# A linear-attention kernel with a rational activation on one core: all steps in a new order, and about twenty steps on other engines

## The chip, the core and the metric

The kernel runs on one core of one Trainium2 chip. Times are device microseconds of one execution. The kernel before took 216.31, 215.97 and 213.47 us in the three runs shown, a median of 215.97 us. The profile is of one further execution.

The engines are named as the profile names them: PE multiplies matrices (PEld is its loading of weights), DVE is VectorE, ACT is ScalarE, POOL is GpSimd, SP only issues transfers. "L500" is line 500 of the kernel's file.

## The reference

For each of 4 batches and 8 heads, a state of 48 x 48 is carried over 768 time steps:

```python
f = 1.0 / (1.0 + np.exp(-f_logit))
for t in range(S):
    state = f[:, :, t, :, None] * state + np.einsum('bhd,bhe->bhde', k[:, :, t], v[:, :, t])
    y[:, :, t] = np.einsum('bhd,bhde->bhe', q[:, :, t], state)
```

The result, as 3072 tokens of 384 numbers (8 heads x 48), goes through two dense layers (384 to 2048 and back) with a rational activation between them:

```python
h = x @ w_in
P = a[0] + a[1] * h + a[2] * h**2 + a[3] * h**3
Q = 1.0 + abs(b[0]) * abs(h) + abs(b[1]) * h**2
out = (P / (Q + 1e-6)) @ w_out
```

## The kernel before

**Units.** The work is cut into 12 units, numbered 0 to 11. Unit n holds 256 time steps (n // 4 says which of three stretches) of batch n % 4, all eight heads. Units of one batch depend on each other through a state in SBUF; the four batches alternate, so there are three other units between a state's update and its next use. Within a unit the 256 steps are two chunks (j = 0, 1) and the heads are four pairs.

**Steps of a unit, attention.** `ld` loads f, k, q (issued by SP) and v (by POOL). `ef` and `ls` (ACT) make the logarithm of the gate; `cs` (PE) sums it over time; `A` (ACT) makes its exponentials; `xa` (DVE) multiplies q (x = 0) and k (x = 1) with them, or `xg` does it on POOL for half of k's heads. `T` (PE) transposes the products and `Te` (ACT, or DVE) copies the transposes to SBUF. `sc` (PE) makes the scores, `mk` (DVE) masks them, `yb` and `yi` (PE) make the attention output y from scores and from the old state, `kv` and `si` (PE) the new state, which `st` (DVE) scales. `vm` (POOL) packs a part of v for `yb`. `ye` copies y from PSUM to the tile xT (ACT with argument s, DVE with v).

**Steps of a unit, dense layers.** `h` (PE) multiplies with w_in, four blocks of 128 columns at a time, so four times a unit; `hy` copies each such group from PSUM to SBUF (ACT, or DVE with v). On the 16 blocks of a unit, DVE then squares (`sq`, L500), takes the absolute value (`ab`, L508), makes two affine forms (`p1`, L542, and `p2`, L547) and the product of one with the square (`pm`, L556). Two sums are left: the denominator's z + h2 and the numerator's g + hy. Each is made in halves of eight blocks (128 partitions x 2048 numbers), and each half in one of three ways: on DVE (`zv` L526, `tv` L564), by a DMA that accumulates in SBUF, issued by POOL (`zd` L530, `ta` L560), or, for some groups of the denominator, by PE (`u` L516). ACT takes the logarithm of the denominator (`ln` from PSUM, `lz` L534 from SBUF) and the exponential of its negative (`ex` L538), which gives 1/Q; DVE multiplies it in (`gm`, L568). `o` (PE, L578) multiplies with w_out, eight groups of four matmuls a unit, `oe` copies the result from PSUM, `so` stores it.

**What sets the order.** Nothing is scheduled. The text ORDER lists every step of all units in one order, and each engine works its own instructions in exactly that order, waiting on semaphores for what they need. `@2` gives the PSUM slot (of four). `>mk.2.0` after a load or an `xg` makes it wait for that other step. `dz` are matmuls without a use, in the first microseconds and at the end. POOL and SP are queues of the same kind: a transfer that waits for its buffer holds up whatever stands behind it. The tiles of q, k, f and v come from pools of three buffers each; a load waits until the last reader of the buffer's former contents is done.

The functions `load` (L184), `xa` (L305), `ye` (L433), `hy` (L493), `zv`, `zd`, `ta`, `tv` (L524 to L564) and `oe` (L581) are those that the steps named in the prediction run through.

Of the kernel before, what the change touches and what calls it, by code (L numbers as in the profile page):

```python
# [19 lines left out]
ld 0 f 2 4; cu 1; cz 0; ab_ b a; ld 0 f 0 2; cz 2; ld 0 k 0 2; cu 0; ld 0 k 2 4; ld 0 q 2 4; ci; cm; dz 9 @0  # L20
ld 0 q 0 2; ld 1 f; ld 0 v; ab_ a s; ld 1 k; fa; ld 1 q; ef 0 2 4; ef 0 0 2; cz 3; ls 0 0 2; ls 0 2 4; cz 1
cs 0 2 4 @2; cs 0 0 2 @3; A 0 0 2 4; dz 4 @0; A 0 1 2 4; xa 0 0 2 4; A 0 1 0 2; xa 0 1 2 4; A 0 0 0 2
xa 0 1 0 2; T 0 2 4 @0; vm 0 1; Te 0 2 4; dz 2 @2; sc 0 1 @0; kv 0 @3; xa 0 0 0 2; mk 0 1; T 0 0 2 @1; fr; ef 1
Te 0 0 2; dz 4 @2; ae 0; ls 1; wi 8 12; si 0 0; sc 0 0 @0; wi 12 16 >ls.1; ld 2 f >mk.0.1; vm 0 0; cs 1 @1
ld 1 v; yb 0 2 4 @2; mk 0 0; wi 4 8; st 0 0; A 1 1; wi 0 4; yb 0 0 2; xa 1 1; yi 0 1; si 0 1; dz 3 @0; A 1 0
xa 1 0; dz 3; st 0 1; ye 0 0 1 v; ye 0 1 3 s; T 1 @1; Te 1 s; vm 1 1; fb; vm 1 0; ld 2 v; h 0 8 12 @2
hy 0 8 12 v; vm 2 1; sc 1 0 @0; ef 2; sc 1 1 @3; vm 2 0; mk 1 1; ha 0 12 16 @1; hb 0 12 16; ld 3 f >ye.0.0.1
ls 2; kv 1 @2; si 1 0; dz 1 @3; cs 2 @3; hy 0 12 16; ae 1; mk 1 0; ld 2 k; yb 1 2 4 @0; ab 0 8 12; ld 3 v
yb 1 0 2; st 1 0; A 2 1; yi 1 1; si 1 1; ld 4 v; sq 0 8 12; A 2 0; h 0 4 8 @1; ye 1 s; ef 3; h 1 12 16 @3
# [12 lines left out]
sq 2 0 16; u 1 0 4 @3; gm 0 0 8; A 5 0; A 5 1; h 3 0 4 @2; wo 4 8; xg 5 1 0 2 >gm.0.0.8; hy 3 8 12; sc 4 1 @1
ln 1 0 4; kv 4 @3; h 3 12 16 @0; hy 3 0 4; ae 4; ex 1 8 16; ld 6 v; mk 4 1; ld 7 f; ld 9 f; ld 5 v; hy 3 12 16
xa 5 0; ef 6; ex 1 0 8; ld 6 k; si 4 0; o 0 0 0 4 @2; sc 4 0 @1; o 0 0 8 12; pm 2 0 16; h 3 4 8 @0; ls 6
xg 5 1 2 4 >pm.2.0.16; hy 3 4 8; mk 4 0; o 0 1 12 16; o 0 1 0 4; st 4 0; yb 4 2 4 @1; ef 7; zv 2 8 16; yi 4 1
yi 4 0; p2 2 0 16; lz 2 8 16; si 4 1; sq 3 0 16; o 0 0 12 16; yb 4 0 2; o 0 1 8 12; st 4 1; cs 6 @0; o 0 1 4 8
ab 3 0 16; o 0 0 4 8; ta 2 0 8; p1 3 0 16; ye 4 s; A 6 1; oe 0 0 2 s; A 6 0; h 4 4 8 @1; tv 1 8 16; T 5 @2
u 2 0 4 @3; hy 4 4 8; vm 6 0; ld 8 f; ef 9; ld 7 k; ld 8 v; h 4 12 16 @0; Te 5 s; ln 2 0 4; h 4 0 4 @1
hy 4 12 16; sc 5 0 @3; hy 4 0 4; h 4 8 12 @2; u 2 4 8 @1; ef 8; kv 5 @0; hy 4 8 12; ln 2 4 8; vm 5 1; pm 3 0 16
sc 5 1 @2; zd 3 0 8; vm 5 0; vm 6 1; si 5 0; so 0 0 2 s; gm 1 0 8; gm 1 8 16; o 1 1 4 8 @1  # L50
xg 6 1 0 2 >gm.1.8.16; mk 5 0; o 1 1 8 12; ae 5; xg 6 1 2 4 >mk.5.0; mk 5 1; ls 7; st 5 0; yi 5 0 @3; p2 3 0 16
ex 2 8 16; cs 7 @2; A 7 1; ld 6 q; ld 7 q; si 5 1; xa 6 0; yb 5 2 4; yb 5 0 2; yi 5 1; o 1 0 12 16; o 1 1 12 16
A 7 0; zv 3 8 16; ab 4 0 16; ex 2 0 8; T 6 @2; o 1 1 0 4; o 1 0 4 8; Te 6 s; ta 3 0 8; o 1 0 0 4; st 5 1
# [54 lines left out]
def kernel(  # L108
# [161 lines left out]
    def ef(n, a0=0, a1=HP):  # L270
        f = unit(n)["f"][:, 2 * a0:2 * a1].rearrange("p h i d -> p (h i d)")
        nc.scalar.activation(f, f, AF.Exp, scale=-1.0)  # L272
# [364 lines left out]
```

## Time and profile before

| | |
|---|---|
| runs shown | 216.31, 215.97, 213.47 us |
| span of the profiled execution (first to last instruction) | 212.2 us |
| the profiled execution's own time beside it | not given; the runs lie 1.3 to 4.1 us above the span |
| busy: PE, DVE, ACT, POOL | 202.0, 200.3, 193.2, 86.5 us |
| mean granted PE clock | 1.000 |
| moved by DMA | 41.10 MB |

A busy time counts from an instruction's start to its end. Neighbours on an engine overlap by a few hundredths of a microsecond, so what one instruction costs an engine without gaps is the distance from its start to the next one's. The ends of matmuls are modelled: one of 128x384 takes 326 ns by its row, but twelve in a row advance PE by 1.95 us. The DMA share of a stretch adds up the queues and can lie above 1.

### The profile page before, as it was taken

How to read it: one execution, taken by the hardware profiler on the slowest of the kernel's cores; microseconds unless marked ns; L12 is line 12 of the kernel's file. 1: busy time of each engine (PE TensorE's matmuls, PEld its weight loads, DVE VectorE, ACT ScalarE, POOL GpSimd, SP SyncE). 2: the span in 40 equal slices, each digit the busy share in tenths (PEclk: the TensorE clock that was granted, in tenths of full speed). 3: DMA queues.
4: the chain of work that ended last, by engine and by line, in shares of the span. 5: the costliest groups of instructions: out<-in, count | busy, mean ns of one | idle time of the engine just before them, and what ended most of it. 6: DMA issues, size and time to landing. Idle time of an engine off the chain costs nothing.

```text
span 212.2 us, 7141 instructions
## 1 busy us (share of the span) xinstructions
PE 202.0 (95%) x3167; PEld 140.4 (66%) x3167; DVE 200.3 (94%) x210; ACT 193.2 (91%) x195; POOL 86.5 (41%) x106
## 2 busy tenths in 40 slices
PE   4999999989999999999999999999999989999993
PEld 1466677557776675677686686686686667676551
DVE  4786989999999999999999999999999999999991
ACT  3565699999999999899999999999999999999990
POOL 6151222661324793633136447397356143133100
PEclk9999999999999999999999999999999999999999
DMA  5999999999899999999299999599997996949924
GB/s 138 244 200 215 233 241 223 255 235 214 152 187 74 237 207 240 259 197 213 73 237 238 238 235 182 97 191 244 201 189 150 186 173 117 198 89 274 204 116 153
DMA packets 60623, 41.10 MB, mean 194 GB/s; under 512 B 51120, under 2 KB 54960, under 8 KB 60592
## 3 DMA queue, kind: packets, MB, share of 16 engines
q0 software_dynamic: 20944, 21.76, 63.5%
q1 hardware_dynamic: 39360, 18.68, 34.1%
q8 instruction: 25, 0.41, 0.8%
q10 hardware_dynamic: 288, 0.20, 0.3%
q14 instruction: 6, 0.05, 0.1%
HBM read 25.17 MB, written 4.72 MB: 141 GB/s over the span
## 4 chain that ended last, share of the span: by engine, by line
PE 18%; ACT 16%; DVE 14%; issue 5%; DMA 4%; ACTq 0%; POOLq 0%
PE op L578 12%; PE hp L460 5%; ACT hy L495 4%; ACT qi L538 4%; DMA z<-h 4%; ACT lq L534 3%; DVE h L500 3%; DVE scm L359 2%; DVE gall L568 2%; ACT qkT L336 1%; DVE gall L542 1%; ACT A L303 1%; DVE z L508 1%; DVE gall L556 1%; DVE gall L564 1%
## 5 line engine op out<-in xcount | busy, mean ns | idle before, releaser
L578 PE MATMUL op<-w_out_sb,gall 128*128 128x384 bf16 x384 | 69.0, 326 | 0.0
L460 PE MATMUL hp<-xT,w_in_sb 128*128 128x256 bf16 x564 | 67.6, 273 | 1.4 <-ACT xT L442 0.7
L460 PEld LDWEIGHTS <-w_in_sb 128*128 128x128 bf16 x564 | 54.3, 98 | 11.2 <-issue 1.5
L578 PEld LDWEIGHTS <-gall 128*128 128x128 bf16 x384 | 36.2, 98 | 22.7 <-DVE gall L568 0.5
L495 ACT CAST hy<-hp 128x1024 bf16<-128x1024 f32 x47 | 49.3, 1090 | 1.1 <-PE hp L489 1.0
L538 ACT ACTIVATE qi<-lq 128x4096 bf16<-128x4096 f32 (+2 forms) x18 | 45.6, 2539 | 0.0
L534 ACT ACTIVATE lq<-z 128x2048 f32<-128x2048 bf16 (+1 forms) x20 | 36.8, 1878 | 0.3 <-DMA z<-h 0.3
L560 POOL DMA_DIRECT2D gall<-hy x18 | 19.3, 1124 | 28.4 <-DVE gall L556 10.8
L359 DVE TENSOR_TENSOR scm<-sc,mask 128x1024 bf16<-128x1024 f32 x24 | 28.8, 1217 | 0.6 <-PE sc L351 0.6
L314 POOL TENSOR_TENSOR qkp<-kn,A 128x384 bf16<-128x384 f32 x17 | 17.0, 1002 | 29.8 <-ACT alast L447 7.4
L500 DVE TENSOR_TENSOR h<-hy 128x4096 bf16<-128x4096 bf16 (+2 forms) x19 | 28.3, 1500 | 0.2 <-ACT hy L495 0.2
L568 DVE TENSOR_TENSOR gall<-gall,qi 128x4096 bf16<-128x4096 bf16 (+2 forms) x17 | 28.2, 1668 | 0.2
L366 POOL COPY vmp<-vn 128x128 bf16<-128x128 bf16 x24 | 20.3, 919 | 19.7 <-DMA vn<-in_v_dram 18.4
L556 DVE TENSOR_TENSOR gall<-gall,h 128x4096 bf16<-128x4096 bf16 (+2 forms) x17 | 28.2, 1665 | 0.0
L530 POOL DMA_DIRECT2D z<-h x15 | 14.9, 1051 | 24.9 <-DVE h L500 7.2
L303 ACT ACTIVATE A<-cs 128x768 f32<-128x768 f32 (+1 forms) x26 | 19.7, 800 | 3.7 <-PE cs L287 2.9
L547 DVE TENSOR_SCALAR hy<-hy,a_sb 128x4096 bf16<-128x4096 bf16 (+1 forms) x14 | 16.7, 1192 | 0.0
L542 DVE TENSOR_SCALAR gall<-hy,a_sb 128x4096 bf16<-128x4096 bf16 (+1 forms) x14 | 16.6, 1187 | 0.0
L508 DVE TENSOR_SCALAR z<-hy 128x4096 uint16<-128x4096 uint16 (+2 forms) x19 | 16.1, 853 | 0.0
L272 ACT ACTIVATE fn<-fn 128x768 f32<-128x768 f32 (+1 forms) x13 | 10.8, 831 | 5.4 <-DMA fn<-in_f_logit_dram 5.4
L194 POOL DMA_DIRECT2D vn<-in_v_dram x12 | 12.9, 1079 | 6.8 <-issue 6.8
L326 PE MATMUL tp<-ident,qkp 128*128 128x128 bf16 x192 | 12.8, 219 | 0.2
(74 smaller groups left out, 266.7 us busy)
## 6 DMA issues: line engine op xcount, KB each, us to landing
gall<-hy POOLq DMA_DIRECT2D x16, 512.0 KB, 7.0
z<-h POOLq DMA_DIRECT2D x13, 512.0 KB, 7.8
fn<-in_f_logit_dram SPq DMA_DIRECT2D x11, 384.0 KB, 8.4
kn<-in_k_dram SPq DMA_DIRECT2D x11, 384.0 KB, 9.4
qn<-in_q_dram SPq DMA_DIRECT2D x11, 384.0 KB, 9.7
out_dram<-osb SPq DMA_DIRECT2D x11, 384.0 KB, 3.5
vn<-in_v_dram POOLq DMA_DIRECT2D x12, 192.0 KB, 7.2
w_in_sb<-in_moe_w_in_dram POOLq DMA_DIRECT2D x4, 384.0 KB, 7.8
```

The costliest lines, as they stand in the source:

```text
L303: nc.scalar.activation(t, src, AF.Exp, scale=1.0 if x else -1.0)
L359: return nc.vector.tensor_mul(t, s["sc", g].rearrange("s r a i t -> s (r a) (i t)"), mb)
L366: nc.gpsimd.tensor_copy(s["vm"][:, :, :, 32 * x:32 * x + 16], src)
L460: nc.tensor.matmul(t[:, m - m0, :], w_in_sb[:, kk, m * P:(m + 1) * P], s["x"][:, kk].rearrange("p i j t -> p (i j t)"), start=(kk == 0), s ...
L495: (nc.scalar.copy if eng == "s" else nc.vector.tensor_copy)(fl(big(s, "hy", "hy", 3), m0, m1), fl(s["hp", m0], 0, m1 - m0))
L500: return nc.vector.tensor_mul(fl(big(s, "h2", "h2", 2), m0, m1), fl(s["hy"], m0, m1), fl(s["hy"], m0, m1))
L534: nc.scalar.activation(fl(lq, m0, m1), fl(s["z"], m0, m1), AF.Ln, scale=regs[2], bias=1.0 + 1e-6)
L538: nc.scalar.activation(fl(qi, m0, m1), fl(lq, m0, m1), AF.Exp, scale=-1.0)
L556: return nc.vector.tensor_mul(fl(s["g"], m0, m1), fl(s["g"], m0, m1), fl(s["h2"], m0, m1))
L560: nc.gpsimd.dma_start(out=fl(s["g"], m0, m1), in_=fl(s["hy"], m0, m1), accum_op=ALU.add)
L568: return nc.vector.tensor_mul(fl(s["g"], m0, m1), fl(s["g"], m0, m1), fl(qi, m0, m1))
L578: nc.tensor.matmul(s["op", j][:, j, 0:DM], s["g"][:, m, P * j:P * j + P], w_out_sb[:, m, :], start=(s["on", j] == 1), stop=(s["on", j] == KF))
```

## The change

The diff replaces the whole of ORDER. It changes no arithmetic function; nine of them now also return their instruction, so that another step may be made to wait for it. One row of ORDER, and one such function:

```diff
-ex 2 8 16; cs 7 @2; A 7 1; ld 6 q; ld 7 q; si 5 1; xa 6 0; yb 5 2 4; yb 5 0 2; yi 5 1; o 1 0 12 16; o 1 1 12 16
+xg 6 1 2 4 >mk.5.0; ae 5; ex 2 8 16; ex 2 0 8; tv 3 8 16; st 5 0; o 1 0 0 4 @1; o 1 1 0 4; o 1 1 12 16
...
     def zd(n, m0, m1):
         s = unit(n)
-        nc.gpsimd.dma_start(out=fl(s["z"], m0, m1), in_=fl(s["h2"], m0, m1), accum_op=ALU.add)
+        return nc.gpsimd.dma_start(out=fl(s["z"], m0, m1), in_=fl(s["h2"], m0, m1), accum_op=ALU.add)
```

Both orders have 824 steps. Taken as a set, without order and slots, they differ in fifteen:

| unit | before | after |
|---|---|---|
| 0 | attention output: first third on DVE, the rest on ACT | both parts on ACT |
| 0 | hidden copy of blocks 8 to 12 on DVE | on ACT |
| 1 | copy of the transposes on ACT | on DVE |
| 1 | sum of g, blocks 8 to 16, on DVE | DMA |
| 2 | sum of z, blocks 8 to 16, on DVE | DMA |
| 2 | sum of g, blocks 8 to 16, on DVE | DMA |
| 3 | sum of z, blocks 8 to 16, on DVE | DMA |
| 3 | sum of g, blocks 8 to 16, by DMA | DVE |
| 4 | sum of g, blocks 8 to 16, on DVE | DMA |
| 5 | sum of z: blocks 0 to 8 by DMA, 8 to 16 on DVE | the other way round |
| 5 | attention output on ACT | DVE |
| 5 | hidden copy of blocks 12 to 16 on ACT | DVE |
| 8 | `xg` of k, first half, waits for unit 5's DVE sum | for unit 5's DMA |
| 11 | copy of the last output's first half on DVE | ACT |

The rest is order. First, DVE between unit 4's first state update and the products that finish unit 1. In the names, z0 and h20 are unit 2's denominator and square, z1 and h21 unit 3's, gall1 unit 1's numerator, qkp the products of q or k. Before:

```order
L451 TENSOR_TENSOR state0_1_97<-sv_1394,alast_1449 128x384
L526 TENSOR_TENSOR z0_617<-z0_617,h20_670 128x2048
L547 TENSOR_SCALAR hy2_1144<-hy2_1144,a_sb_104 128x4096
L500 TENSOR_TENSOR h21_760<-hy0_471 128x4096
L451 TENSOR_TENSOR state0_0_96<-sv_1394,alast_1449 128x384
L508 TENSOR_SCALAR z1_807<-hy0_471 128x4096
L542 TENSOR_SCALAR gall0_705<-hy0_471,a_sb_104 128x4096
L564 TENSOR_TENSOR gall1_916<-gall1_916,hy1_709 128x2048
L556 TENSOR_TENSOR gall0_705<-gall0_705,h21_760 128x4096
L568 TENSOR_TENSOR gall1_916<-gall1_916,qi_91 128x2048 x2
```

The same place after; the first and the last row are unit 5's and unit 6's product of q:

```order
L314 TENSOR_TENSOR qkp1_88<-qn_1377,A_89 128x2x8x48
L500 TENSOR_TENSOR h21_763<-hy0_496 128x4096
L451 TENSOR_TENSOR state0_0_96<-sv_1400,alast_1457 128x384
L508 TENSOR_SCALAR z1_761<-hy0_496 128x4096
L547 TENSOR_SCALAR hy2_1130<-hy2_1130,a_sb_104 128x4096
L542 TENSOR_SCALAR gall0_718<-hy0_496,a_sb_104 128x4096
L568 TENSOR_TENSOR gall1_933<-gall1_933,qi_91 128x2048
L314 TENSOR_TENSOR qkp0_87<-qn_1648,A_89 128x2x8x48
```

Both sums (L526, L564) have left DVE, and unit 6's product of q stands six steps behind unit 5's; before, seventeen steps stood between those two. The two sums are now on POOL's queue. Before, its queue at about this time, where kn_1030 is k of unit 5 and vn_1452, vn_1692 and vn_1460 are v of units 6, 8 and 5:

```order
L314 TENSOR_TENSOR qkp1_88<-kn_1030,A_89 128x2x4x48
L560 DMA gall2_1333<-hy2_1144 128x2048
L366 COPY vmp0_94<-vn_1452 128x8x16
L194 DMA vn_1692<-in_v_dram 128x8x96
L366 COPY vmp1_95<-vn_1460 128x8x16
```

After, where vn_1323, vn_887 and vn_1461 are v of units 5, 4 and 7:

```order
L194 DMA vn_1323<-in_v_dram 128x8x96
L366 COPY vmp0_94<-vn_887 128x8x16
L530 DMA z0_714<-h20_683 128x2048
L560 DMA gall1_933<-hy1_712 128x2048
L194 DMA vn_1461<-in_v_dram 128x8x96
L366 COPY vmp1_95<-vn_1323 128x8x16
```

The load of v and the copies now stand behind two issues of sums. Third, SP's queue, with the semaphores that a load waits for in brackets. Before, around units 6 and 7:

```order
L194 DMA kn_1690<-in_k_dram 128x8x96 [waits DMAHW4_49,DVE_49,Pool_49]
L591 DMA out_0_dram<-osb_1646 128x768 [waits DMAHW5_49,Activation_49]
L194 DMA qn_1870<-in_q_dram 128x8x96
L194 DMA qn_1872<-in_q_dram 128x8x96 [waits DMAHW7_49]
L194 DMA kn_2075<-in_k_dram 128x8x96 [waits DMAHW0_49,Pool_49]
```

After, from unit 8's q (qn_756) on; qn_758, qn_1377, qn_1379 and qn_1648 are q of units 4, 5, 7 and 6:

```order
L194 DMA qn_756<-in_q_dram 128x8x96 [waits DMAHW4_49]
L194 DMA qn_758<-in_q_dram 128x8x96 [waits DMAHW5_49,DVE_49]
L194 DMA kn_1375<-in_k_dram 128x8x96 [waits DMAHW6_49,DVE_49]
L194 DMA qn_1377<-in_q_dram 128x8x96 [waits DMAHW7_49,DMAHW0_49,DVE_49]
L194 DMA qn_1379<-in_q_dram 128x8x96 [waits DMAHW5_49,DVE_49]
L194 DMA fn_1381<-in_f_logit_dram 128x8x96 [waits DMAHW1_49,Activation_49]
L194 DMA fn_1454<-in_f_logit_dram 128x8x96 [waits DMAHW2_49,Activation_49]
L194 DMA qn_1648<-in_q_dram 128x8x96 [waits DMAHW7_49,DMAHW3_49,DVE_49]
```

Unit 8's q is loaded ahead of unit 4's and keeps its buffer until unit 8. Unit 6's q waits for DVE, for unit 5's product of q, whose buffer it takes over; before it had no such wait when its turn came.

More of the change, by code (lines that the diff above doesn't have):

```diff
@@ L25 @@
[L25 to L29, printed above, removed]
@@ new lines @@
+ln 1 4 8; sq 2 0 16; p1 2 0 16; ab 2 0 16; gm 0 0 8; T 4 @0; A 5 1; hy 3 8 12; zd 2 8 16; pm 2 0 16; Te 4 s
+u 1 0 4 @1; h 3 0 4 @2; ln 1 0 4; ld 5 k; ld 5 q; ld 7 q; ld 6 f; sc 4 1 @0; kv 4 @3; h 3 12 16 @1; ld 7 f
+hy 3 0 4; ae 4; ex 1 8 16; ta 1 8 16; ld 7 v; o 0 1 4 8 @2; hy 3 12 16; vm 5 0; vm 4 1; o 0 0 4 8; si 4 0
+o 0 1 8 12; sc 4 0 @1; o 0 0 8 12; ex 1 0 8; mk 4 1; st 4 0; mk 4 0; vm 5 1; xg 5 1 2 4 >pm.2.0.16
+xg 5 1 0 2 >gm.0.0.8; h 3 4 8 @0; ef 6; hy 3 4 8; o 0 1 12 16; o 0 0 12 16; yb 4 2 4 @1; yb 4 0 2; yi 4 0; yi 4 1
@@ new lines @@
+o 5 1 12 16; o 5 0 8 12; o 5 1 4 8; o 5 1 8 12; A 11 1; ae 10; ye 9 s; h 9 8 12 @0; si 10 0; p1 8 0 16
+h 9 0 4 @1; lz 7 0 8; oe 5 0 2 s; st 10 0; T 10 @2; hy 9 8 12; hy 9 0 4; h 9 4 8 @3; Te 10 s; p2 8 0 16
+gm 6 0 16; lz 7 8 16; sc 10 1 @0; h 9 12 16 @2; ta 7 8 16; zd 8 8 16; ta 7 0 8; vm 11 0; zd 8 0 8
+xg 11 1 0 2 >gm.6.0.16; sc 10 0 @1; mk 10 1; mk 10 0; pm 8 0 16; hy 9 4 8; yb 10 2 4 @0; yi 10 1
+xg 11 1 2 4 >mk.10.1; hy 9 12 16; T 11 @3; yb 10 0 2; ta 8 0 8; ta 8 8 16; yi 10 0; ex 7 0 16; ye 10 s; Te 11 s
@@ new lines @@
+kv 11 @2; o 6 1 8 12 @1; si 11 0; o 6 0 12 16; o 6 0 0 4; o 6 1 4 8; o 6 1 12 16; sq 9 0 16; ab 9 0 16; gm 7 0 16
+o 6 1 0 4; o 6 0 4 8; sc 11 0 @0; o 6 0 8 12; zd 9 0 8; ae 11; lz 8 8 16; lz 8 0 8; mk 11 0; h 10 0 4 @3
+oe 6 0 2 s; ex 8 0 16; vm 11 1; p1 9 0 16; st 11 0; sc 11 1 @0; zd 9 8 16; h 10 4 8 @1; yi 11 0 @2; yi 11 1
+yb 11 0 2; mk 11 1; yb 11 2 4; hy 10 0 4; h 10 8 12 @0; o 7 1 8 12 @3; ye 11 s; h 10 12 16 @2; p2 9 0 16
+pm 9 0 16; ta 9 8 16; ta 9 0 8; hy 10 8 12; hy 10 4 8; gm 8 0 16; hy 10 12 16; ab 10 0 16; sq 10 0 16
@@ new lines @@
+o 8 0 0 4; o 9 1 12 16; o 9 1 8 12; o 9 0 12 16; pm 11 8 12; o 8 1 0 4; zd 11 8 12; hy 11 0 4; lz 11 8 12
+zd 11 12 16; gm 10 0 16; ex 11 8 12; oe 8 0 2 s; lz 11 12 16; pm 11 12 16; dz 1 @3; o 9 0 8 12; ta 11 8 12
+sq 11 4 8; sq 11 0 4; ab 11 4 8; o 10 0 8 12 @3; o 10 0 4 8; o 10 0 12 16; o 10 1 4 8; u 11 4 8 @0; o 10 1 8 12
+o 10 1 0 4; so 7 0 2 s; so 8 0 2 s; ab 11 0 4; p1 11 0 8; zv 11 0 4; ta 11 12 16; pm 11 4 8; gm 11 8 12
+pm 11 0 4; ln 11 4 8; o 10 0 0 4; o 10 1 12 16; o 11 0 8 12 @0; o 11 1 8 12 @2; ex 11 12 16; p2 11 0 8
@@ L99 @@
+gm 11 12 16; ex 11 4 8; lz 11 0 4; tv 11 4 8; so 5 0 2 s; gm 11 4 8; o 11 0 12 16; o 11 1 12 16; tv 11 0 4
+oe 10 0 2 s; ex 11 0 4; o 11 0 4 8; o 11 1 4 8; gm 11 0 4; oe 9 0 2 s; o 11 0 0 4; so 10 0 2 s; o 11 1 0 4
+oe 11 0 1 s; oe 11 1 2 s; so 9 0 2 s; so 11 0 1 s; so 11 1 2 a
 """
@@ L271, in ef @@
         f = unit(n)["f"][:, 2 * a0:2 * a1].rearrange("p h i d -> p (h i d)")
-        nc.scalar.activation(f, f, AF.Exp, scale=-1.0)
+        return nc.scalar.activation(f, f, AF.Exp, scale=-1.0)
     def ls(n, a0=0, a1=HP):
@@ L494, in hy @@
         s = unit(n)
-        (nc.scalar.copy if eng == "s" else nc.vector.tensor_copy)(
+        return (nc.scalar.copy if eng == "s" else nc.vector.tensor_copy)(
             fl(big(s, "hy", "hy", 3), m0, m1), fl(s["hp", m0], 0, m1 - m0))
@@ L559, in ta @@
         s = unit(n)
-        nc.gpsimd.dma_start(out=fl(s["g"], m0, m1), in_=fl(s["hy"], m0, m1), accum_op=ALU.add)
+        return nc.gpsimd.dma_start(out=fl(s["g"], m0, m1), in_=fl(s["hy"], m0, m1), accum_op=ALU.add)
     def tv(n, m0, m1):
```

138 lines of the change are left out of this document (60 added, 78 removed).

## The prediction

> **What bounds the kernel now.** I read the page's head first, then the busy time of each engine in stretches, then the chain of waits, then the groups of instructions and the transfers. The head says that no engine is to spare:
>
> ```profile
> span 212.2 us, 7141 instructions
> PE 202.0 (95%) x3167; PEld 140.4 (66%) x3167; DVE 200.3 (94%) x210; ACT 193.2 (91%) x195; POOL 86.5 (41%) x106
> ```
>
> The stretches (microseconds; then PE, PEld, DVE, ACT, POOL, granted clock, DMA share, GB/s) say when:
>
> ```profile
> 10.00:20.00 10.00, 9.08 (x228) 6.13 (x232) 7.70 (x14) 5.64 (x9) 4.16 (x7) 1.00 1.23 210
> 20.00:30.00 10.00, 9.94 (x203) 7.79 (x192) 9.61 (x14) 7.16 (x10) 1.36 (x3) 1.00 1.29 228
> ...
> 70.00:80.00 10.00, 10.00 (x101) 7.71 (x100) 10.00 (x8) 10.00 (x12) 8.69 (x7) 1.00 1.14 233
> 80.00:90.00 10.00, 9.92 (x199) 6.05 (x198) 10.00 (x11) 9.04 (x11) 5.58 (x5) 1.00 1.09 247
> ```
>
> Slack lies in the head: in the first two rows ACT is idle for 4.4 and 2.8 us and DVE for 2.3 and 0.4. After that three engines run without a gap, and the clock is full. The chain, in order of time (start, length, what), has three legs:
>
> ```profile
> 116.27 2.20 DVE h L500
> ...
> 120.15 7.83 DMA z<-h
> ...
> 144.16 1.99 ACT hy L495 x2
> ...
> 169.93 1.17 ACT hy L495
> ...
> 171.14 1.47 PE hp L460 x12
> ...
> 208.66 0.56 DVE osb L585
> ```
>
> To about 120 us it runs through DVE, from there to 171 us through ACT, and from 171.1 to 208.6 us through PE alone. Its PE work is the same after the change, so PE's leg can begin earlier but not shrink. A gain on DVE counts until ACT is next, and ACT's own gain limits the second leg.
>
> **Half sums.** The change turns five sums on DVE into accumulating DMAs (z of units 2 and 3, g of units 1, 2 and 4, upper halves) and one DMA (g of unit 3) back into a DVE sum: net four. One swaps its half (z of unit 5) and costs nothing net. Groups, with busy time and mean ns of one:
>
> ```profile
> L564 DVE TENSOR_TENSOR gall<-gall,hy 128x2048 bf16<-128x2048 bf16 x6 | 7.4, 1254 | 0.0
> L526 DVE TENSOR_TENSOR z<-z,h 128x2048 bf16<-128x2048 bf16 x4 | 4.9, 1218 | 0.0
> ...
> L495 ACT CAST hy<-hp 128x1024 bf16<-128x1024 f32 x47 | 49.3, 1090 | 1.1 <-PE hp L489 1.0
> L442 ACT ACTIVATE xT<-y 128x768 bf16<-128x768 f32 x11 | 9.5, 866 | 0.0
> L495 DVE CAST hy<-hp 128x1024 bf16<-128x1024 f32 x1 | 1.2, 1226 | 1.6 <-PE hp L460 1.6
> L441 DVE TENSOR_SCALAR xT<-y,sig 128x256 bf16<-128x256 f32 x1 | 0.5, 480 | 0.0
> L585 ACT COPY osb<-op 128x384 f32<-128x384 f32 x1 | 0.5, 478 | 1.7 <-PE op L578 1.7
> L585 DVE COPY osb<-op 128x384 f32<-128x384 f32 x1 | 0.6, 557 | 1.6 <-PE op L578 1.6
> ```
>
> A neighbour starts some 0.08 us before the last one ends (rows below: 68.80 + 1.33 against 70.06), so a sum is worth 1.22 - 0.08 = 1.14 us: 4 x 1.14 = 4.6 us off DVE.
>
> What the sums cost elsewhere: four more issues on POOL and four more transfers. The transfer rows (KB each, median us to landing), the load of q, one window's k, and one pair of q:
>
> ```profile
> gall<-hy POOLq DMA_DIRECT2D x16, 512.0 KB, 7.0
> z<-h POOLq DMA_DIRECT2D x13, 512.0 KB, 7.8
> ...
> q0 software_dynamic: 20944, 21.76, 63.5%
> ...
> DMA to landing us min/median/max: 4.4/9.0/12.5
> ...
> kn<-in_k_dram SPq DMA_DIRECT2D x1, 384.0 KB, 5.9
> ...
> qn<-in_q_dram SPq DMA_DIRECT2D x2, 384.0 KB, 9.8
> ```
>
> The tightest of the new sums is unit 1's. It is issued behind unit 2's z, when DVE has done the absolute value of unit 2, and DVE does twelve steps before the product that needs it: 14 us by the start-to-start times below. Two issues of about 0.9 us and a landing of 10 us make 12. So it is hidden with 2 us to spare; each microsecond over that would stand on DVE. Units 2 and 4 have 17 and 18 us. ACT's two new waits (logarithm of units 2 and 3) stand behind nine or more of its steps, most of them as long as a hidden copy (1.0 us). Behind the new pair on POOL are the load of v for unit 7 and the copies for units 4 and 5; POOL is 41% busy, and I take no wait from it.
>
> **Steps that change engine.** In the middle, unit 5 gives DVE its attention output (128x768) and one hidden copy (128x1024). For the first DVE has no row; between the 128x256 row (480 ns) and the 128x1024 row (1226 ns) a line gives 0.98, bounds 0.48 and 1.23; I take 0.98, less 0.08. The second is 1.15. DVE's middle is thus 4.6 - 0.9 - 1.15 = **2.5 us** shorter. ACT loses 0.87 + 1.09 less two overlaps (the chain has two copies in 1.99 us, so 1.0 for one of 1.09): **1.8 us**. At the end the last two output copies both go to ACT; the first is covered by PE's last four products, the second is 0.48 instead of 0.56: -0.1. The store of unit 9 now also goes out there, 0 to +0.6; I take 0.
>
> **Head.** Rows of DVE and PE:
>
> ```profile
> 17.37 0.74 DVE L260 TENSOR_SCALAR a_sb<-a_sb,sig 128x3 f32<-128x3 f32 x3
> 19.72 1.23 DVE L495 CAST hy<-hp 128x1024 bf16<-128x1024 f32 x1 [1.61 <-PE hp L460]
> 20.86 2.35 DVE L359 TENSOR_TENSOR scm<-sc,mask 128x1024 bf16<-128x1024 f32 x2
> ...
> 16.67 1.06 PE L326 MATMUL tp<-ident,qkp 128*128 128x128 bf16 x16
> 18.21 1.47 PE L460 MATMUL hp<-xT,w_in_sb 128*128 128x256 bf16 x12 [0.48 <-ACT xT L442]
> ```
>
> ScalarE alone now copies unit 0's output, and earlier, which saves DVE 0.4 us and ACT the wait between the parts. But the three coefficient steps (0.7 us) now stand ahead of unit 1's products, so unit 1's transposes begin at 17.2 instead of 16.7 and the first hidden block follows them at 18.25, against 18.21. DVE then copies the transposes (1.2 us) instead of that block (1.2 us), and its two masks end at about 23.1, as now. I count 0; bounds -0.9 and +0.9, from the coefficient steps and a rounding of 0.2 us either way.
>
> **The load of unit 6's q.** The new order loads unit 8's q ahead of unit 4's, which keeps one of three buffers occupied for long; unit 6's q now waits for the buffer that unit 5's product frees. Between that product and unit 6's, DVE has six steps; their pace now:
>
> ```profile
> 68.80 1.33 DVE L547 TENSOR_SCALAR hy<-hy,a_sb 128x4096 bf16<-128x4096 bf16 x1
> 70.06 2.28 DVE L500 TENSOR_TENSOR h<-hy 128x4096 bf16<-128x4096 bf16 x1
> 72.26 0.55 DVE L451 TENSOR_TENSOR state<-sv,alast 128x384 bf16<-128x384 f32 x1
> 72.73 1.65 DVE L508 TENSOR_SCALAR z<-hy 128x4096 uint16<-128x4096 uint16 x1
> 74.30 1.33 DVE L542 TENSOR_SCALAR gall<-hy,a_sb 128x4096 bf16<-128x4096 bf16 x1
> ```
>
> Square 2.20, state 0.47, absolute value 1.13 to 1.57, the two affine steps 1.26 and 1.25, and a half product of about 1.14: 7.5 us. The load needs about 0.3 us to be issued. With 5.9 us to landing, as the k load shows in the window from 67 us, there is no wait; with 9.8, as the pair of q at 73.95, DVE stands 2.6. The load is first in its burst, but two sums and a load of v are in flight. I take the middle, 7.9: **+0.7 us**; ends 0 and 12.5 + 0.3 - 7.5 = 5.3.
>
> **Sum.** DVE: -2.5 + 0.7 = -1.8. ACT: -1.8. On each leg the smaller counts, so -1.8 + 0 (head) - 0.1 (end) = -1.9. The profiled execution would go from a span of 212.2 to 210.3 us. The page has no time for it but the span, which lies 3.8 us below the median of the runs shown (215.97, of 213.47 to 216.31). Added to the median: **214.1 us**, 0.9% less.
>
> **A rule weighed.** The row first, durations min/median/max of DVE's absolute value and of POOL's issue of a sum:
>
> ```profile
> L508 DVE TENSOR_SCALAR z<-hy x19: 416/720/1649, 23.1 to 198.0; 128x4096 uint16<-128x4096 uint16 x9, 128x1024 uint16<-128x1024 uint16 x8, 128x2048 uint16<-128x2048 uint16 x2
> ...
> L560 POOL DMA_DIRECT2D gall<-hy x18: 852/941/2044, 39.6 to 198.3; - x18
> ```
>
> One full step in nine is stretched, by 0.4 us, at 72.73, where POOL is issuing a load. If every new issue stopped DVE for its whole 0.94 us, four would cost 3.8 us: DVE comes to -2.5 + 0.7 + 3.8 = +2.0, and the time to 215.97 + 2.0 - 0.1 = 217.9. As a rival this gets 0.04, since one row in nine is stretched at all. The Trainium skill, "SBUF — State Buffer", section "Who interferes with whom", says this of two-port DVE modes: whichever of DVE and GpSimd comes first holds the shared ports for its whole instruction. By that rule the rival's full price would be due; the trace agrees in one step and not in the others.
>
> **Rivals.**
> - *The q load comes late (slower).* At 10.7 to 12.5 us DVE stands 3.5 to 5.3. From a landing of 9.7 on it eats the whole 2.5, and above that the kernel is slower: 217 to 218.8. For it: DMA shares over 1 from 70 us on. Against: at 67 to 70 us loads landed in 5 to 6 us. 0.15.
> - *The transfers become the bound.* The software queue takes 0.635 x 212.2 / 21.76 = 6.2 us per MB; four sums of 0.52 MB add 13 us of all engines, between 45 and 130 us, where little is free. If a third of that shows, 220. Against: shares over 1 are queues that overlap, and almost no compute step waits for a transfer after the head. 0.06.
> - *Nothing comes through.* Steps put in another order make PE, which has no gap in its rows, wait elsewhere, or the change's savings fall beside work: 215.9. 0.22.
> - *More than the sum.* The new order also closes the 1 us of ACT's gap in the 80 to 90 row and 1 to 2 us of the head, and all of DVE's 2.5 counts: 215.97 - 2.5 - 1 - 1 to 2 = 210.5 to 211.5. 0.15.
>
> **Numbers.** The forecast (213 to 215.3) has 0.38. A tenth on each side is left out: 211.0 to 218.6 reaches most of the fast case, all of the late load, and leaves the transfer case out. Two per cent (4.3 us) is about what a measurement of this kernel tells from no change; it needs 211.65 or 220.3. Faster by that: the fast case's 0.15 less a quarter, and a little of the forecast: 0.13. Slower: the transfer case and the worst of the late load, 0.08. Within: 0.79.
>
> **What would show it.** Right: fewer DVE sums (L526 and L564 together 9 instead of 13), DVE busy about 197 us, ACT about 192, the same PE leg of 37 us at the end begun 1 to 2 us earlier, and a short idle time of DVE before unit 6's product, put down to the transfer of q. A long one there, or waits of DVE's products and ACT's logarithms for transfers, would make it wrong, as would a span shorter by 4 us, which would say that I misread the head.

## The result, and the profile after

The changed kernel takes 216.19 us (median of 17 runs, 214.54 to 218.95), the kernel before 214.57 us beside it (17 runs, 213.2 to 216.95). A ratio, here and below, takes only runs within about 1.5% of their version's fastest (16 of the 17 here, 9 of 12 for E2, 4 of 5 for E5, 4 of 13 for E9). The ratio is **1.0069, 95% interval 1.004 to 1.0098**: 0.7% slower, where 0.9% faster was forecast. The profiled execution has a span of 214.7 us, against 212.2.

The page's head, after:

```profile
span 214.7 us, 7145 instructions
PE 201.1 (94%) x3167; PEld 141.3 (66%) x3167; DVE 200.3 (93%) x206; ACT 193.9 (90%) x195; POOL 92.9 (43%) x110
```

DVE has four instructions fewer (206 for 210) and exactly the same busy time, 200.3 us. The sums have gone (the two groups for L526 and L564 on half units now count 2 and 4, before 4 and 6), so other steps must have become longer: by the rows of the steps that left or joined DVE (four half sums -4.9, two small copies -1.0, unit 5's output and unit 1's transposes +2.2) it should have lost 3.7 us. ACT's busy time did not fall either (193.9 us, before 193.2). POOL is busier by 6.4 us. The groups by shape, after (busy time, mean ns of one):

```profile
L547 DVE TENSOR_SCALAR hy<-hy,a_sb 128x4096 bf16<-128x4096 bf16 x10 | 14.6, 1462 | 0.0
L542 DVE TENSOR_SCALAR gall<-hy,a_sb 128x4096 bf16<-128x4096 bf16 x10 | 14.1, 1412 | 0.0
```

The two had means of 1345 and 1339 ns before: 1.9 us more over twenty instructions, about half of what is missing. Next, POOL's products of k (`xg`, one line of the code), durations in ns as min/median/max, before:

```profile
L314 POOL TENSOR_TENSOR qkp<-kn,A x17: 995/1000/1024, 37.3 to 158.9; 128x384 bf16<-128x384 f32 x17
```

and after:

```profile
L314 POOL TENSOR_TENSOR qkp<-kn,A x17: 992/1000/4919, 38.8 to 162.0; 128x384 bf16<-128x384 f32 x17
```

They never took more than 1.02 us and now take up to 4.92. The stretches say where time is lost (columns as in the prediction). Two of them before:

```profile
50.00:60.00 10.00, 9.90 (x166) 7.58 (x166) 10.00 (x11) 10.00 (x14) 2.73 (x4) 1.00 1.05 180
90.00:100.00 10.00, 9.85 (x140) 7.38 (x139) 10.00 (x9) 10.00 (x10) 3.74 (x4) 1.00 1.18 207
```

and after:

```profile
50.00:60.00 10.00, 8.65 (x151) 6.29 (x149) 10.00 (x10) 7.62 (x10) 4.61 (x1) 1.00 1.22 223
90.00:100.00 10.00, 8.42 (x133) 7.12 (x129) 9.43 (x9) 8.47 (x10) 7.21 (x9) 1.00 1.16 242
```

Two places: around 55 to 60 us ACT stands 2.4 us and PE 1.3, around 90 to 100 us ACT, PE and DVE stand 1.5, 1.6 and 0.6. The first place, in order of time on POOL, DVE, ACT and PE (start, length; in brackets the idle time before and what ended it):

```profile
55.39 4.92 POOL L314 TENSOR_TENSOR qkp<-kn,A 128x384 bf16<-128x384 f32 x1 [10.57 <-ACT lsp L277]
...
55.18 0.94 DVE L314 TENSOR_TENSOR qkp<-qn,A 128x768 bf16<-128x768 f32 x1
56.05 1.21 DVE L568 TENSOR_TENSOR gall<-gall,qi 128x2048 bf16<-128x2048 bf16 x1
57.18 2.27 DVE L500 TENSOR_TENSOR h<-hy 128x4096 bf16<-128x4096 bf16 x1
59.38 2.01 DVE L542 TENSOR_SCALAR gall<-hy,a_sb 128x4096 bf16<-128x4096 bf16 x1
...
60.34 0.81 ACT L303 ACTIVATE A<-cs 128x768 f32<-128x768 f32 x1 [2.23 <-POOL qkp L314]
...
60.37 0.51 PE L326 MATMUL tp<-ident,qkp 128*128 128x128 bf16 x6 [1.55 <-POOL qkp L314]
```

Before, the same product of unit 4 ran beside a mask, which has one of its two inputs in PSUM:

```profile
52.05 1.00 POOL L314 TENSOR_TENSOR qkp<-kn,A 128x384 bf16<-128x384 f32 x1 [6.19 <-ACT A L303]
...
51.55 1.22 DVE L359 TENSOR_TENSOR scm<-sc,mask 128x1024 bf16<-128x1024 f32 x1
```

In both orders this `xg` carries the mark `>tv.1.0.8`: it begins when unit 1's half sum is done. Before, the mask `mk 3 0` stood behind that sum on DVE; now there stand unit 4's product of q, half of unit 0's last product and unit 2's square, all with two inputs in SBUF. The mark was kept, and what it led to was moved. POOL came to its end 0.9 us after the square's, while the next affine step took 2.01 us instead of 1.34.

The second place, in SP's queue and then on ACT:

```profile
71.55 0.37 SPq L194 DMA_DIRECT2D qn<-in_q_dram  x1
72.01 1.67 SPq L194 DMA_DIRECT2D kn<-in_k_dram  x2
73.77 4.25 SPq L194 DMA_DIRECT2D fn<-in_f_logit_dram  x2
...
92.54 0.85 ACT L272 ACTIVATE fn<-fn 128x768 f32<-128x768 f32 x1 [1.07 <-DMA fn<-in_f_logit_dram]
93.85 0.85 ACT L272 ACTIVATE fn<-fn 128x768 f32<-128x768 f32 x1 [0.46 <-DMA fn<-in_f_logit_dram]
```

Unit 6's q waits for unit 5's product (ended at 71.5), and behind it k of units 6 and 8 and f of units 9 and 8, all with the three half sums at 75.6 to 78.8 us. The second of the f loads was 17.1 us under way (76.73 to 93.83 in the chain of waits). Unit 6's q itself landed in 5.3 us, and DVE did not wait for it.

The chain of waits of this execution runs through both places (start, length, what):

```profile
55.39 4.93 POOL qkp L314
...
76.73 17.10 DMA fn<-in_f_logit_dram
```

Between them and behind them, to 113 us, it is mostly on ACT, then on PE to 156 and on ACT again to 197 us. The three legs of the chain before (DVE, ACT, and PE for the last 37 us) are not found in it.

### The profile page after: what moved, and what is told of

The parts are those of the page before. It is cut to its first block, busy times and chain, and to the rows that moved or that the text cites. A ratio compares the mean times of both kernels' runs of the same rounds, so it can differ in the third digit from the quotient of the medians.

```text
span 214.7 us, 7145 instructions
## 1 busy us (share of the span) xinstructions
PE 201.1 (94%) x3167; PEld 141.3 (66%) x3167; DVE 200.3 (93%) x206; ACT 193.9 (90%) x195; POOL 92.9 (43%) x110
## 4 chain that ended last, share of the span: by engine, by line
ACT 30%; PE 27%; DMA 16%; issue 12%; DVE 7%; POOL 4%; SPq 2%; ACTq 0%; POOLq 0%
PE op L578 13%; DMA fn<-in_f_logit_dram 11%; ACT qi L538 7%; ACT hy L495 7%; PE hp L460 7%; ACT lq L534 7%; DMA kn<-in_k_dram 5%; POOL qkp L314 2%; PE y L373 2%; SPq L194 2%; ACT qkT L336 2%; DVE h L500 2%; ACT xT L442 2%; ACT fn L272 1%; ACT osb L585 1%
## 5 line engine op out<-in xcount | busy, mean ns | idle before, releaser
L578 PE MATMUL op<-w_out_sb,gall 128*128 128x384 bf16 x384 | 68.1, 326 | 0.7 <-ACT hy L495 0.3
L495 ACT CAST hy<-hp 128x1024 bf16<-128x1024 f32 x47 | 48.2, 1072 | 1.2 <-PE hp L489 0.6
L560 POOL DMA_DIRECT2D gall<-hy x20 | 21.8, 1122 | 38.8 <-DVE hy L547 17.0
L314 POOL TENSOR_TENSOR qkp<-kn,A 128x384 bf16<-128x384 f32 x17 | 25.6, 1510 | 23.9 <-ACT lsp L277 14.1
L500 DVE TENSOR_TENSOR h<-hy 128x4096 bf16<-128x4096 bf16 (+2 forms) x19 | 29.1, 1541 | 0.0
L530 POOL DMA_DIRECT2D z<-h x17 | 17.0, 1018 | 22.2 <-DVE z L508 6.8
L303 ACT ACTIVATE A<-cs 128x768 f32<-128x768 f32 (+1 forms) x26 | 19.0, 784 | 4.9 <-PE cs L287 2.6
L194 POOL DMA_DIRECT2D vn<-in_v_dram x12 | 15.1, 1257 | 7.9 <-issue 4.0
L547 DVE TENSOR_SCALAR hy<-hy,a_sb 128x4096 bf16<-128x4096 bf16 (+1 forms) x14 | 17.8, 1277 | 0.0
L366 POOL COPY vmp<-vn 128x128 bf16<-128x128 bf16 x24 | 10.2, 505 | 12.8 <-DMA vn<-in_v_dram 11.0
```

The source lines that it names most:

```text
L194: i = eng.dma_start(out=s[what][:, hh].rearrange("p h i d -> p h (i d)"), in_=src[s["b"], hh, t0:t0 + NT, :].rearrange("h (p i) d -> p h ( ...
L314: return eng.tensor_mul(s["qk"][:, :, x, hh, 0:D], s["qk"[x]][:, hh].rearrange("p h i d -> p i h d"), A_sb[:, :, x].rearrange("p i (h d) - ...
L495: return (nc.scalar.copy if eng == "s" else nc.vector.tensor_copy)(fl(big(s, "hy", "hy", 3), m0, m1), fl(s["hp", m0], 0, m1 - m0))
L500: return nc.vector.tensor_mul(fl(big(s, "h2", "h2", 2), m0, m1), fl(s["hy"], m0, m1), fl(s["hy"], m0, m1))
L560: return nc.gpsimd.dma_start(out=fl(s["g"], m0, m1), in_=fl(s["hy"], m0, m1), accum_op=ALU.add)
L578: nc.tensor.matmul(s["op", j][:, j, 0:DM], s["g"][:, m, P * j:P * j + P], w_out_sb[:, m, :], start=(s["on", j] == 1), stop=(s["on", j] == KF))
```

## The experiments

Theory A: POOL's products are held off by DVE's steps with two SBUF inputs, then stretch the step behind them. Theory B: unit 6's late q holds other loads back. All ratios are against the kernel before, with 95% intervals, from 5 to 13 runs of each version.

**E1, two marks.**

```diff
-xg 4 1 2 4 >tv.1.0.8
+xg 4 1 2 4 >pm.1.0.8
-xg 6 1 0 2 >gm.1.8.16
+xg 6 1 0 2 >p2.3.0.16
```

> The changed kernel with two marks moved: POOL's product of unit 4's k begins behind DVE's half product of unit 1 (that is, beside a mask), no longer behind unit 1's half sum; the one of unit 6 behind unit 3's second affine step, no longer behind unit 1's last product. Nothing else differs. Theory A (POOL's product is held off while DVE runs steps with two SBUF inputs, and ACT and PE wait for it at 58 to 60 us): the two products take 1.0 us instead of 4.9 and 3.8, ACT's wait of 2.2 us and PE's of 1.6 for them fall under 0.5, the two DVE steps stretched to 2.0 us are 1.34 again, and the ratio to the kernel before falls from 1.007 to 0.998 (0.995 to 1.001). Theory B (the loads held back on SP's queue by unit 6's q are the cause): the products get shorter all the same, but the time is made up before 100 us; ratio 1.004 to 1.008.

Measured: **0.9997 [0.9965, 1.003]**. Unit 4's product takes 1.00 us, unit 6's 1.00 (3.79 without the edit). POOL's products, as above:

```profile
L314 POOL TENSOR_TENSOR qkp<-kn,A x17: 992/1001/1962, 39.1 to 160.0; 128x384 bf16<-128x384 f32 x17
```

and the longest waits of ACT from 30 to 200 us (in total, times, longest):

```profile
ACT fn L272 <- DMA fn<-in_f_logit_dram: 1.6, 1, 1.6
ACT A L303 <- PE cs L287: 0.5, 1, 0.5
```

ACT's wait for POOL is gone. The two marks are worth the whole loss against the kernel before. ACT's wait for f is still there, at 1.56 us in one piece. What held POOL is still there too, but now it holds a copy of unit 4's v, which comes next on POOL and for which nobody waits (from the order of time):

```profile
54.39 5.53 POOL L366 COPY vmp<-vn 128x128 bf16<-128x128 bf16 x1
```

The same copy takes 1.17 us in the changed kernel, at 61.88. So not the hold costs, but whom it holds.

**E2, unit 8's q later.**

```diff
-ld 8 q; ld 4 q; hy 0 0 4
+ld 4 q; hy 0 0 4
...
-ld 9 q; ld 10 q
+ld 8 q; ld 9 q; ld 10 q
```

> The changed kernel with one load moved back: unit 8's q is loaded just ahead of unit 9's, as before the change, not ahead of unit 4's. Theory B (SP's queue): unit 6's q no longer waits for unit 5's product, so f of units 9 and 8 goes out more than 5 us earlier, ACT's waits for f at 92 to 94 us (1.07 and 0.46 us) go, and the ratio falls from 1.007 to 0.999 (0.996 to 1.002). Theory A (ports): POOL's product of unit 4's k still takes over 3 us, ACT's wait for it stays near 2.2 us, and the ratio stays at 1.004 to 1.008.

Measured: 1.0045 [1.0003, 1.0087]. The waits for f are gone, the wait for POOL is not; ACT's longest waits (as above):

```profile
ACT A L303 <- POOL qkp L314: 2.3, 1, 2.3
ACT hy L495 <- PE hp L460: 0.8, 2, 0.5
```

The ratio lies in A's band, but its interval overlaps that of the changed kernel, so by time E2 alone settles nothing on B. (Its profiled execution is 2.5 us behind the changed kernel's at unit 1's first state update already, 25.96 against 23.49 us, with a granted clock of 0.83 at 20 to 30 us; only waits and durations are read from it. From unit 3's first state update to unit 11's it takes 122.9 us, the changed kernel 123.9.)

**E3, both edits.**

> Both edits in one kernel: the two marks moved, and unit 8's q loaded ahead of unit 9's. If A and B each hold half of the loss, the ratio is 0.992 (0.988 to 0.996), which is the gain that was forecast for the change (0.991). If only one holds, it equals that one's kernel, about 0.998. If neither, 1.004 to 1.008.

Measured: **0.9942 [0.9906, 0.9977]**, faster than the kernel before. Against E1 the one edit of E2 is worth 0.55% here, with no wait of ACT for f left. The start of DVE's first state update (L451) of a unit, read from the order of time, shows where each edit gains (E8 is below; the orders of these four are the same on DVE):

| unit | after | E1 | E3 | E8 |
|---|---|---|---|---|
| 3 | 49.25 | 49.56 | 49.44 | 48.97 |
| 4 | 67.38 | 66.56 | 66.44 | 65.97 |
| 5 | 87.30 | 86.00 | 85.89 | 85.25 |
| 6 | 101.49 | 99.47 | 98.98 | 98.34 |
| 11 | 173.10 | 171.09 | 170.51 | 169.73 |

Counted from unit 3, E1 gains 1.1 us by unit 4 and 0.5 more by unit 5, where the two products stood, 0.7 by unit 6 (from what, was not followed), and nothing after. E3 gains 0.4 more between units 5 and 6, where the waits for f stood. Both theories hold; how they share is not settled (by the table 2.3 and 0.5 us, by the ratios 0.7% and 0.55%, that is 1.5 and 1.2 us).

**E4, the half sums alone, in the old order.** Steps taken out of the kernel before and put in, each new DMA issued where DVE has made its inputs:

```diff
-zv 2 8 16; tv 1 8 16; tv 2 8 16; zv 3 8 16; tv 4 8 16; ta 3 8 16
+zd 2 8 16; ta 1 8 16; ta 2 8 16; zd 3 8 16; ta 4 8 16; tv 3 8 16
```

> The kernel before with the four half sums alone (upper halves of z of units 2 and 3 and of g of units 1, 2 and 4 as DMAs, of unit 3's g back on DVE), in the old order otherwise. Theory C (the sums as such pay, and the rest of the new order eats it): DVE's busy time falls by 4 to 5 us to about 196, ACT is next, ratio 0.994 (0.990 to 0.999). Theory D (the four more transfers congest the queues): loads land later, ACT waits for f or logarithms for sums, ratio 1.003 to 1.015. Nothing: 0.999 to 1.002, where ACT and PE set the pace and DVE's gain turns into idle time.

Measured: **1.0627 [1.057, 1.0684]**, far outside all three. DVE's busy time did fall, to 197.8 us, but in the order of time DVE stands before one product:

```profile
95.66 0.96 DVE L314 TENSOR_TENSOR qkp<-qn,A 128x768 bf16<-128x768 f32 x1 [9.25 <-DMA qn<-in_q_dram]
```

In the old order unit 6's q is loaded late, at 75.4 us, among the sums; it was 20 us under way. PE stood nearly still from 90 to 100 us; in the columns of the stretches above:

```profile
90.00:100.00 10.00, 2.43 (x19) 2.18 (x20) 4.34 (x4) 3.14 (x3) 0.00 (x0) 0.64 1.20 224
```

The granted clock, 1.00 before, is 0.64 here and 0.85 from 100 to 110 us: PE stopped at about 88.7 us, and in stretches of 2 us the clock is 0.50 from 94 to 102 us, when PE is at work again. So of the 13 us that E4 loses, 9.25 are DVE's wait, and a part of the rest is work at a lower clock, which followed the wait. All six runs show a mean clock of 0.968 to 0.977.

**E5, the same with q of units 6 and 7 loaded behind unit 6's k.**

```diff
-A 7 1; ld 6 q; ld 7 q; si 5 1
+A 7 1; si 5 1
...
-ld 6 k; si 4 0
+ld 6 k; ld 6 q; ld 7 q; si 4 0
```

> The kernel with the four half sums in the old order, with one more edit: the loads of q of units 6 and 7 stand directly behind the load of unit 6's k, some 20 us earlier on SP's queue than in the old order (they need no store and no other load first). The kernel without this edit took 1.063 and its DVE stood 9.25 us for unit 6's q, 20 us under way among the sums. Theory E (the sums crowd the transfers only where q is loaded late, which is what the new order's early loads are for): DVE's wait for q goes, ratio 0.990 to 1.003. Theory D (the sums congest wherever they are): the wait moves to other loads, ratio above 1.02.

Measured: 1.0096 [1.0053, 1.0138]. The wait for q is gone, the clock stays at 1.00 there, and 5.3% of the time is saved, so theory E's mechanism holds; its number does not. DVE stands 2.05 us for scores of unit 5 at 83.7 us and 0.7 to 0.9 in three other places, and ACT 1.60 us at 130.6 and 0.98 at 49.9. The four sums need an order that loads early and spaces the rest; that part of the new order has a use. What each of E5's small waits comes from was not followed further.

**E6, the collision alone, in the old order.**

```diff
-tv 1 0 8; xg 4 1 2 4 >tv.1.0.8; mk 3 0
+tv 1 0 8; mk 3 0
...
-xa 4 1 0 2; yb 3 2 4
+xa 4 1 0 2; xg 4 1 2 4 >xa.4.1.0.2; yb 3 2 4
```

> The kernel before with one step moved: POOL's product of unit 4's k begins behind DVE's product of the other half of k (at 54.9 us in the old order, where DVE then has a product with two SBUF inputs of 1.1 us and an affine step), not beside the mask at 51.6 us. Theory A (POOL is held off by DVE's steps with two SBUF inputs, then shares with the affine step): the product takes 2.0 us (1.7 to 2.3) instead of 1.0, the affine step behind it 2.0 us instead of 1.34, PE's transposes wait 1.2 to 1.8 us, ratio 1.005 (1.001 to 1.009). If POOL is not held off: 1.0 us for the product, 1.34 for the affine step, PE waits 0.4 us, ratio 0.998 to 1.002.

Measured: 1.0023 [0.9992, 1.0054]. The mechanism came as expected, the price did not; POOL, DVE and PE in order of time:

```profile
54.62 1.91 POOL L314 TENSOR_TENSOR qkp<-kn,A 128x384 bf16<-128x384 f32 x1 [6.60 <-DVE qkp L314]
...
54.46 1.22 DVE L568 TENSOR_TENSOR gall<-gall,qi 128x2048 bf16<-128x2048 bf16 x1
55.59 2.02 DVE L542 TENSOR_SCALAR gall<-hy,a_sb 128x4096 bf16<-128x4096 bf16 x1
57.54 1.41 DVE L508 TENSOR_SCALAR z<-hy 128x4096 uint16<-128x4096 uint16 x1
...
56.59 0.51 PE L326 MATMUL tp<-ident,qkp 128*128 128x128 bf16 x6 [0.56 <-POOL qkp L314]
```

POOL is held for the rest of the product (to 55.7) and then runs beside the affine step, which takes 2.02. PE had ten other transposes to do first and waits 0.56 us, not 1.2 to 1.8. A short collision costs DVE 0.7 us and little else; by time alone E6 is inconclusive.

**E7, E3 with the half sums as before the change.** The reverse of E4's diff, in place.

> The version with both edits (marks moved, unit 8's q later; 0.994) with the half sums as before the change: upper halves of z of units 2 and 3 and of g of units 1, 2 and 4 on DVE again, unit 3's g by DMA again, each at the same place in the order. If the sums' term holds in the new order (4 x 1.14 = 4.6 us of DVE, DVE without idle time from 40 us on), the ratio goes from 0.994 to 1.010 (1.003 to 1.017) and DVE's busy time from 198 to 203. If the sums' gain is hidden behind ACT and PE: 0.993 to 0.998.

Measured: **1.0212 [1.0175, 1.0249]**. DVE's busy time goes from 198.3 to 203.0 us, 4.7 us, beside the forecast term of 4.6 (4.9 if the overlaps of neighbours are left in, as in a busy time). The time goes up by more, 2.7% (5.8 us): the sums have two SBUF inputs too, and POOL's copies of v and its products are held by them (three copies took 1.60 us in E3), until PE and ACT stand. POOL and ACT in order of time:

```profile
61.88 4.77 POOL L366 COPY vmp<-vn 128x128 bf16<-128x128 bf16 x3 [1.06 <-DVE z L508]
66.64 2.90 POOL L314 TENSOR_TENSOR qkp<-kn,A 128x384 bf16<-128x384 f32 x2
...
71.49 1.01 ACT L495 CAST hy<-hp 128x1024 bf16<-128x1024 f32 x1 [4.18 <-PE hp L460]
```

PE stands too, from about 66 to 69 us, and the granted clock is then 0.50 from 70 to 72 us (mean of the execution 0.991, of E3's 1.000). How much of the 5.8 us is the sums, how much the collisions and how much the clock, E7 does not separate.

**E8, E3 with two more collisions taken out.**

```diff
-xg 6 1 0 2 >p2.3.0.16; zd 3 0 8; mk 5 0
+xg 6 1 0 2 >p2.3.0.16; mk 5 0
-xg 6 1 2 4 >mk.5.0; ae 5
+xg 6 1 2 4 >mk.5.0; zd 3 0 8; ae 5
...
-xg 8 1 2 4 >mk.7.1
+xg 8 1 2 4 >xa.8.0
-xg 8 1 0 2 >zd.5.8.16
+xg 8 1 0 2 >xa.8.0
```

> The version with both edits (0.994) with two more collisions taken out: POOL issues unit 3's lower sum of z behind, not between, its two products of unit 6's k, so that the second runs beside a mask and not beside a half sum (stretched to 1.89 us); and its two products of unit 8's k begin behind unit 8's product of q, one mask earlier (now 2.94 us, with an affine step stretched to 1.83). Theory A: DVE's half sum is 1.21 again and the affine step under 1.6, about 1.0 us less on DVE; ratio 0.990 (0.986 to 0.994). Rival (these collisions are hidden): 0.992 to 0.997.

Measured: **0.9911 [0.9878, 0.9945]**, 212.77 us against 214.87: it beats both kernels. Its affine steps, by shape:

```profile
L547 DVE TENSOR_SCALAR hy<-hy,a_sb 128x4096 bf16<-128x4096 bf16 x10 | 13.7, 1375 | 0.0
L542 DVE TENSOR_SCALAR gall<-hy,a_sb 128x4096 bf16<-128x4096 bf16 x10 | 13.4, 1342 | 0.0
```

and POOL's products:

```profile
L314 POOL TENSOR_TENSOR qkp<-kn,A x17: 989/1000/1882, 38.6 to 158.6; 128x384 bf16<-128x384 f32 x17
```

The one of 1.88 us that is left stands beside an affine step (see the last section). By the table it is ahead of E3 by 0.5 us at unit 3 already, which neither edit touches, and gains 0.2 us by unit 5 and 0.15 behind unit 7, near the places of the edits: in time E8 lies in A's band and just outside the rival's, which its interval overlaps, so only that the stretched steps are short again is shown, not that they were worth a whole microsecond.

**E9, E1 with the loads of k and f ahead of unit 6's q.**

```diff
-ld 6 q; ld 6 k; h 4 4 8 @1; u 2 0 4 @3; ld 8 k; ld 9 f; ld 8 f
+ld 6 k; h 4 4 8 @1; u 2 0 4 @3; ld 8 k; ld 9 f; ld 6 q; ld 8 f
```

> The changed kernel with the two marks moved (0.9997) and, on SP's queue, the loads of k of units 6 and 8 and of f of unit 9 put ahead of the load of unit 6's q; unit 8's q is still loaded ahead of unit 4's and keeps its buffer. Theory B (what stands behind the held load is what costs): f of unit 9 is issued before 66 us instead of at 73 us, ACT's wait of 1.6 us for f goes, and the ratio is that of the version with unit 8's q loaded later, 0.994 (0.991 to 0.998). If the buffer that unit 8's q keeps is what costs, by the late load of unit 6's q itself: 0.998 to 1.002, with DVE or PE waiting near unit 6's product of q.

Measured: 1.0027 [0.9982, 1.0071]. Its runs scatter from 213.55 to 226.61 us. The profiled execution is one of the long ones; DVE in it:

```profile
88.22 0.96 DVE L314 TENSOR_TENSOR qkp<-qn,A 128x768 bf16<-128x768 f32 x1 [10.85 <-DMA qn<-in_q_dram]
```

The first f was issued at 63.3 us and not waited for; but unit 6's q, now in the middle of the burst, took 18.2 us to land (that this landing makes the scatter is likely, but only one execution was profiled). PE stands in that execution from 85 to 94 us, and the granted clock is 0.50 from 92 to 100. So it is not the queue behind the held load that costs as such: in these versions, with one of three buffers kept by unit 8's q, some load is late, and the order on SP says which.

**E10, E8 with unit 5's two steps on ACT again.**

```diff
-ye 5 v
+ye 5 s
-hy 5 12 16 v
+hy 5 12 16
```

> The version with all four edits (0.991) with unit 5's attention output and its last hidden copy on ACT again, as before the change: DVE loses 0.9 + 1.15 us there, ACT gains 1.8 us. By the forecast's three legs (ACT sets the pace from 120 us on) the version gets slower by what ACT gains less what PE and DVE let pass, 0.5 to 1.8 us: ratio 0.996 (0.993 to 1.000). By the rival (DVE, without idle time from 40 to 180 us, sets the pace all the way): faster by up to 2.0 us, ratio 0.983 to 0.990.

Measured: **1.0099 [1.0068, 1.013]**, 1.9% above E8 for 1.8 us of ACT. That rules out the rival, by which DVE alone sets the pace. DVE, relieved of two steps, stands instead; two rows of its order of time:

```profile
98.52 1.23 DVE L359 TENSOR_TENSOR scm<-sc,mask 128x1024 bf16<-128x1024 f32 x1 [1.56 <-PE sc L351]
102.46 1.23 DVE L508 TENSOR_SCALAR z<-hy 128x4096 uint16<-128x4096 uint16 x1 [2.71 <-ACT hy L495]
```

In E10 ACT is on the path at 95 to 105 us already, and the price is more than the steps' own length. ACT also stands 1.71 us for a sum at 131.6; whether that is the rest was not tried.

## Why the prediction was wrong

*Half sums (4 x 1.14 = 4.6 us off DVE): right.* E7 measures 4.7 us of busy time (4.9 on that count). L526 and L564 fell from 13 to 9 as said.

*Steps that change engine: the price was right, the place of ACT's leg not.* The attention output took 1.00 us on DVE (0.98 forecast). E10 shows that ACT's relief counts, and, with those two steps back on ACT, from some 95 us on, not from 120. In the changed kernel's own chain ACT comes behind POOL's product at 60 us, and the PE leg of 37 us at the end, which was to stay, is not there; what the legs would be without collisions, the chains do not settle. "Three engines run without a gap" was not so from 30 to 50 us before either, where PE stood 0.8 and 1.1 us in ten.

*Head (0): right.* Unit 1's first state update begins at 23.49 us, before at 23.45.

*The load of unit 6's q (+0.7 us on DVE): the step that was looked for at the wrong waiter.* The load was issued when it was said to be, and first in its burst it landed in 5.3 us, so DVE did not wait. I priced the one who needs the load and not those that stand behind it on SP's queue: f of units 9 and 8, at 1.5 us of ACT; E1 to E3 gives 0.55%. E4 and E9 show that the stall I described is real where the load goes out late or not first, and larger than my bound of 5.3 us: 9.25 and 10.85.

*"POOL is 41% busy, and I take no wait from it", and the rule weighed at 0.04: the step that failed.* ACT and PE did wait for POOL, 2.23 and 1.55 us at one of its products. The rule should have been asked of POOL's products, not of its issues. The row that I quoted for it counted DVE's absolute values beside an issue. The Trainium skill, "SBUF — State Buffer", section "Who interferes with whom", has the case by name: a DVE instruction with two SBUF inputs contends with a GpSimd instruction that reads SBUF, and the ports that they share are an exclusive lock. The trace agrees in kind: 4.92 us for a product of 1.0. In the part-by-part sum there was no term for the `xg` steps, because their marks stood unchanged in the list of differences; what each mark led to on DVE had changed. The missing term is what E1 shows: 0.7% of the time, 2.3 us by the table. The kernel before had the sign, on POOL's copies of v rather than its products (durations in ns as above):

```profile
L366 POOL COPY vmp<-vn x24: 283/324/3589, 9.8 to 170.2; 128x128 bf16<-128x128 bf16 x24
```

The longest is eleven times the median; it began at 139.2 us, beside an affine step and a whole product of DVE.

*Sum.* The forecast ratio was 214.1 / 215.97 = 0.991. E3 has 0.9942, E8 0.9911. So the forecast fits the new order with E8's four edits, and misses the collisions and the late loads, 1.6% between E8 and the changed kernel; that it fits so closely is partly chance, as E8's place in the table shows.

*Transfers become the bound (0.06): no in the new order; in the old one a late load is.* E4 lost 6.3% to it and to the lower clock that followed.

*Nothing comes through (0.22).* This rival was nearest in kind, since it has PE waiting elsewhere in the new order; it did not name for whom, and put the loss at nothing.

## What to carry to other kernels

When steps are put in another order, read for every step that begins behind a mark what now runs beside it, also where the mark's own text is the same. POOL's SBUF work belongs beside DVE steps that read PSUM (here masks: 1.0 us), not beside a row of products. And of a load that must wait, price those who stand behind it on its queue before the one that needs it.

## What was not expected of the hardware

- Three DVE steps with two SBUF inputs in a row, each starting as the last ends, held POOL's product through both boundaries: it took 4.92 us, and 0.9 us of it lay behind the last of them. E1's copy of 0.3 us took 5.53 beside four of them and the end of a fifth. The Trainium skill's section named above speaks of one instruction. POOL can also get in between: in E7 three copies in a row took 1.25, 1.28 and 2.35 us, each to the end of the DVE step that it met and no further, and the two half sums and the product there took 1.30 and 2.37 us instead of 1.21 and 2.28. What decides between the two, no run here shows.
- Two SBUF inputs are not needed for it. In the changed kernel POOL's product at 143.50 us took 1.88 beside an affine step, which has one input in SBUF, begun at 143.19 and 1.33 long; 0.86 us of the product lay behind it. The same pair reads 1.88 in E8 (140.12 us).
- It goes both ways: where POOL began first, DVE's step was the longer one. E3's half sum begun 0.5 us into a product of POOL took 1.89 us instead of 1.21. An affine step with one input took 2.01 instead of 1.34 beside 0.9 us of POOL, which had been waiting longer.
- One load of 384 KB takes 5.3 us when first in its burst and 17 to 20 us among several others and two or three half sums (f of unit 8 in the changed kernel, q of unit 6 in E4 and E9).
- A wait of PE can cost twice. Where PE stood for some microseconds, the granted clock afterwards was 0.50 for 2 to 8 us: 94 to 102 us in E4, 92 to 100 in E9, 70 to 72 in E7. In the changed kernel, whose longest wait of PE shown is 1.55 us, it stays at 1.00 from 50 to 64 and from 88 to 104 us.
